# Eight weight chunks converted in the second stage of the last batch, one instruction per scheduler item

## The chip, the cores and the metric

The kernel runs on one core of a Trainium2 chip. TensorE (PE) multiplies matrices and loads its weights beside that (PEld); VectorE (DVE), ScalarE (ACT) and GpSimd (POOL) do the elementwise work; SyncE (SP) issues all the DMAs, in its program's order. Each engine works through its own instructions in order. The time of a run is the device time of the core in microseconds (us); lower is better.

## The reference, cut to what matters

Three layers follow each other. `B, S` are 4 and 576, the width is 512.

```python
# 1 attention: 4 batches, 8 heads, 1152 keys, 64 wide; queries pooled by two
q_pool = q.reshape(B, H, S // 2, 2, D).mean(axis=3)
attn = softmax(q_pool @ k.T / 8);  x = attn @ v
# 2 four experts, each a causal attention with one head; the two best by the gate are added
logits = x @ w_gate
out += gate[..., e] * (softmax(causal(x @ wq[e] @ (x @ wk[e]).T / 8)) @ (x @ wv[e]) @ wo[e])
# 3 feed-forward with a shifted input
xk = mu_k * x + (1 - mu_k) * x_prev;  xr = mu_r * x + (1 - mu_r) * x_prev
k = np.maximum(xk @ w_k, 0.0);  v = k * k @ w_v;  r = sigmoid(xr @ w_r)
out = r * v
```

`w_k` (512x1024), `w_r` (512x512) and `w_v` (1024x512) come as float64.

## The kernel before

Every matrix product is made of three: a float32 operand is split into a high part and a low part, and high x high, high x low and low x high are added in PSUM.

The float64 weights are first made into such pairs. `w3_split` cuts them into 20 chunks of 128x512 numbers: 8 of `w_k`, 4 of `w_r`, and 8 of `w_v`, which are numbers 12 to 19. A chunk is one load of 512 KB into a tile `w3st` (`ld`); seven DVE instructions and two ACT instructions that build the high and the low part from the bits (`sp1`, `sp2`; lines 884 to 902, with the copy and the difference in the helpers' lines 145 and 71); and two stores of 256 KB to DRAM, `w3h` and `w3l` (line 905). There is one `w3st` buffer, so the load of a chunk waits until both stores of the chunk before it have been read out.

The first part of the program runs the attention of 32 heads (8 a batch; `s1_job`, `s1_max`, `s1_prep`), and beside it the experts of the batch before (`s2_qk`, `s2_max`, `s2_job`, `s2_out`). The nth head of a batch always has the same second-stage work beside it. Then comes the second stage of the last batch, alone with the feed-forward of the first group of 256 rows (`s2_vproj`, the gate, `s2_qk`, `s2_job`, `h_steps`). Then the third stage goes through nine groups of 256 rows: `s3_h` (tile `sth`), `s3_r` (`str`), `s3_v` (`stw`). `s3_v` reads `w_v` from the tiles `wqk_h`, `wqk_l` and `XH`, `XL`, which hold other data until the second stage is over; rows 0 to 3 of `w_v` go to the first two, rows 4 to 7 to the other two, by `w3_load` (lines 1072 and 1073).

The order comes about in two steps. `drive` walks over steps and calls, between them, what each `Task` has due: a `Task` has a start, an end and a list of items, which are spread evenly between the two. What is recorded in that order is then ordered by a scheduler that fills an engine's free places with later work that is ready. So an item can stand well ahead of its place in the list, as far as its inputs and its buffer allow; and within one item nothing says that its instructions stay together.

The names of the second stage, in the order of its work: `stv` is the projection of the values, `stq` that of queries and keys (ACT and DVE make `QA`, `KA`, `QB`, `KB` from it; for every second expert these are the tiles `wvg_h`, `wvg_l`, `QB2b`, `KB2b`), `PM` the row maxima, `nm` their negative, `st` the scores, `p` their exponentials, `U` the sum over the values, `sd`, `rd`, `scr`, `R` the way of the softmax sum through DRAM and back, `YH` and `YL` the result, and `sto` its projection.

Of the kernel before, what the change touches and what calls it, by code (L numbers as in the profile page):

```python
# [55 lines left out]
def tile_kernel(ctx: ExitStack, tc: tile.TileContext, q, k, v, w_gate, wq, wk, wv, wo,  # L56
                mu_k, mu_r, w_k, w_v, w_r, out):
    nc = tc.nc
    LAG, LO, HB = G["LAG"], G["LO"], G["HB"]
    eng = {"g": nc.gpsimd, "v": nc.vector, "s": nc.scalar}  # L60

    def copy(e, dst, src):
        if e == "s":
            nc.scalar.activation(dst, src, AF.Copy)  # L64
        elif e == "v":
            nc.vector.tensor_copy(dst, src)
        else:
# [62 lines left out]
    def f32(ap):  # L130
        return ap.bitcast(F32)
# [12 lines left out]
    def act_hi(dst, src):  # L144
        nc.scalar.activation(dst, src, AF.Copy)
# [14 lines left out]
    def later(n, fn):  # L160
        pending.append((now[0] + n, fn))
# [82 lines left out]
    def normaliser(U, gate, name):  # L244
# [8 lines left out]
        def mid():  # L253
# [49 lines left out]
    def s2_gate(b):  # L303
# [3 lines left out]
        def f():  # L307
# [22 lines left out]
            def g():  # L330
# [247 lines left out]
    NF = G["NF"]  # L578
# [284 lines left out]
    CW = G["CW"]  # L863

    def w3_split(first, end, pool, bufs):
        def chunk(src, n):
            cell = {}

            def ld():
                t = pool.tile([P, max(1280, 5 * G["CW"])], F32, tag="wst", name=f"w3st{n}", bufs=bufs)  # L870
                cell["t"] = t
                if n < 2 and G["blk"]:
                    nc.gpsimd.tensor_copy(t[0:1, 0:1], XT[0:1, G["blk"] - 1, 0:1])
                nc.sync.dma_start(t[:, : 2 * CW].bitcast(I32), src.bitcast(I32))

            def sp1():
# [12 lines left out]
                nc.vector.tensor_scalar(si, ai, -0x800000, None, op0=ALU.bitwise_and)
                if G["wt"] == "g":  # L890
                    nc.gpsimd.tensor_scalar(s, s, 2.0**-36, 0.0, op0=ALU.mult, op1=ALU.add)
                    nc.gpsimd.tensor_tensor(s, low, s, op=ALU.mult)
                else:
                    nc.vector.scalar_tensor_tensor(s, low, 2.0**-36, s, op0=ALU.mult, op1=ALU.mult)
# [103 lines left out]
    n = len(steps)  # L998
# [201 lines left out]
    LAG, LO = G["L2"], G["O2"]  # L1200
# [27 lines left out]
    for e in range(E - 1):  # L1228
        i = ix[marks[e]]
# [59 lines left out]
```

## Time and profile before

| | |
|---|---|
| median of 3 runs | 1118.49 us (1116.62 to 1121.4) |
| the profiled execution | 1109.82 us |
| its span, first to last instruction | 1108.1 us |
| PE busy | 93% |
| DVE busy | 77% |
| ACT, POOL busy | 49%, 38% |
| mean granted TensorE clock | 0.991 |

The profiled execution is a single one, and 8.67 us below the median. Its stages, by the first instruction of each: the first part from 0 to 775 us, the second stage of the last batch to 861, the third stage to the end. PE and DVE are both almost always busy in the first part. In the third stage PE is busy without a break, and DVE half of the time.

### The profile page before, as it was taken

Reading aid. Unit: us, or ns where it says so; the run is one execution under the profiler, and the core shown is the slowest. Engines: PE = TensorE matmul, PEld = TensorE weight load, DVE = VectorE, ACT = ScalarE, POOL = GpSimd, SP = SyncE. Lnnn points to the kernel's source line nnn. Section 1 sums busy time; section 2 is a strip of 40 time slices with the busy share of each in tenths; the row PEclk is TensorE's granted clock in tenths of the full one; section 3 lists DMA queues with packets and bytes.
Section 4 is the critical chain, followed back from the end, with each engine's and each line's share of the span. In section 5 each row is a group of like instructions: output and inputs, shape, how many; then the busy total and the mean of one; then the engine's idle time right before and its main releaser. Section 6 shows DMA issues by size and latency. Waiting matters only on the chain.

```text
span 1108.1 us, 18899 instructions
## 1 busy us (share of the span) xinstructions
PE 1033.5 (93%) x6800; PEld 906.4 (82%) x6800; DVE 855.6 (77%) x1664; ACT 548.1 (49%) x922; POOL 420.7 (38%) x378
## 2 busy tenths in 40 slices
PE   5999999999999889999998889998999999999998
PEld 4788888888888888878878878886887888888887
DVE  5899998899889989999999989897555444444442
ACT  5567666556555455655655546656245212222222
POOL 7343328346444554453566346346100111111110
PEclk9999999999999999999999999999999999999999
DMA  4656545445544554545455445415405021111100
GB/s 113 149 151 145 128 114 128 100 128 153 129 109 116 152 135 125 149 134 135 100 143 158 126 116 130 127 54 182 150 1 182 31 81 39 39 39 39 39 20 20
DMA packets 129099, 119.29 MB, mean 108 GB/s; under 512 B 63751, under 2 KB 91358, under 8 KB 129006
## 3 DMA queue, kind: packets, MB, share of 16 engines
q1 hardware_dynamic: 129006, 118.08, 40.4%
q8 instruction: 54, 0.88, 0.3%
q14 instruction: 39, 0.32, 0.1%
HBM read 63.24 MB, written 20.07 MB: 75 GB/s over the span
## 4 chain that ended last, share of the span: by engine, by line
PE 56%; DVE 27%; DMA 7%; ACT 4%; issue 4%; POOL 1%; SPq 1%; DVEq 0%; ACTq 0%; POOLq 0%
PE stw L1122 9%; PE sth L1086 8%; DVE PM L732 7%; PE str L1109 5%; PE bank L730 5%; PE st L760 4%; PE st L761 4%; PE bank L795 3%; PE bank L797 3%; PE bank L796 3%; PE stq L354 3%; PE bank L788 2%; DVE pl L71 2%; PE bank L498 2%; DVE QA L151 1%
## 5 line engine op out<-in xcount | busy, mean ns | idle before, releaser
L71 POOL TENSOR_TENSOR pl<-p,ph 128x576 fp32r<-128x576 f32 x152 | 234.7, 1550 | 231.4 <-ACT ph L64 159.5
L732 DVE TENSOR_REDUCE PM<-bank 128x1 f32<-128x384 f32 (+1 forms) x480 | 251.9, 543 | 18.6 <-PE bank L730 15.0
L768 ACT ACTIVATE p<-st 128x576 f32<-128x576 f32 x288 | 185.6, 649 | 103.0 <-PE st L761 98.2
L730 PE MATMUL bank<-KA,QA 128*128 128x384 f32 (+1 forms) x480 | 180.4, 389 | 19.5 <-DVE PM L732 9.3
L64 ACT ACTIVATE ph<-p 128x576 fp32r<-128x576 f32 x238 | 162.7, 686 | 61.6 <-PE bank L796 51.9
L760 PE MATMUL st<-QA,KA 128*128 128x288 f32 x576 | 177.7, 319 | 4.5 <-ACT p L768 2.0
L761 PE MATMUL st<-QB,KB 65*128 65x288 f32 x576 | 167.3, 305 | 1.2 <-DMA QB<-mr 1.1
L797 PE MATMUL bank<-pl,VV 128*65 128x288 f32 x480 | 142.3, 297 | 8.4 <-DVE pl L71 6.1
L795 PE MATMUL bank<-ph,VV 128*65 128x288 f32 x480 | 144.7, 302 | 3.1 <-DVE PM L732 1.2
L796 PE MATMUL bank<-ph,VV 128*64 128x288 f32 x480 | 141.6, 295 | 0.0
L760 PEld LDWEIGHTS st<-QA,KA 128*128 128x128 f32 x576 | 111.0, 193 | 14.2 <-ACT p L768 5.6
L730 PEld LDWEIGHTS bank<-KA,QA 128*128 128x128 f32 (+1 forms) x480 | 87.4, 185 | 36.8 <-DVE PM L732 16.0
L761 PEld LDWEIGHTS st<-QB,KB 65*128 65x128 f32 x576 | 110.6, 193 | 4.1 <-DMA QB<-mr 2.0
L1025 POOL TENSOR_SCALAR yxr<-x,omr 128x256 f32<-128x256 f32 x36 | 25.6, 725 | 194.2 <-DVE xkl L151 136.0
L1086 PE MATMUL sth<-xkh,wk 128*128 128x256 f32 x512 | 90.9, 279 | 0.0
L1093 ACT ACTIVATE relu<-sth 128x512 f32<-128x512 f32 x32 | 17.4, 597 | 129.1 <-PE sth L1086 129.1
L71 DVE TENSOR_TENSOR pl<-p,ph 128x576 fp32r<-128x576 f32 x88 | 78.1, 888 | 1.6 <-ACT ph L64 0.7
L1086 PEld LDWEIGHTS sth<-xkh,wk 128*128 128x128 f32 x512 | 78.5, 188 | 0.4
L797 PEld LDWEIGHTS bank<-pl,VV 128*65 128x65 f32 x480 | 65.3, 136 | 12.6 <-DVE pl L71 7.7
L795 PEld LDWEIGHTS bank<-ph,VV 128*65 128x65 f32 x480 | 66.0, 138 | 7.9 <-DVE PM L732 3.0
L1086 PE MATMUL sth<-xkl,wk 128*128 128x256 f32 x256 | 71.4, 279 | 0.0
L796 PEld LDWEIGHTS bank<-ph,VV 128*64 128x64 f32 x480 | 65.2, 136 | 6.0
(209 smaller groups left out, 2336.5 us busy)
## 6 DMA issues: line engine op xcount, KB each, us to landing
KA<-sk SPq DMA_DIRECT2D x60, 160.0 KB
qr<-in_q_dram SPq DMA_DIRECT2D x32, 288.0 KB
kr<-in_k_dram SPq DMA_DIRECT2D x32, 288.0 KB
VF<-in_v_dram SPq DMA_DIRECT2D x32, 288.0 KB
KA<-sk SPq DMA_DIRECT2D x60, 128.0 KB
R<-scr SPq DMA_DIRECT2D x48, 144.0 KB
w3h<-w3st SPq DMA_DIRECT2D x20, 256.0 KB
w3l<-w3st SPq DMA_DIRECT2D x20, 256.0 KB
```

The lines of the kernel that those rows point to most:

```text
L64: nc.scalar.activation(dst, src, AF.Copy)
L71: eng[e].tensor_tensor(dst, src, hi.bitcast(F32), op=ALU.subtract)
L730: nc.tensor.matmul(ps[:n, : 3 * P], QA[i][:, t0 : t0 + n], KA[i][:, 3 * g * P : 3 * (g + 1) * P], start=True, stop=True)
L732: nc.vector.tensor_reduce(pm[:n, c, g : g + 1], ps[:n, : 3 * P], axis=AX.X, op=ALU.max)
L760: nc.tensor.matmul(st[:, n, :HT], KA[i][:, ks], QA[i][:, cs], start=True, stop=False)
L761: nc.tensor.matmul(st[:, n, :HT], KB[i][0 : D + 1, ks], QB[i][0 : D + 1, cs], start=False, stop=True)
L768: nc.scalar.activation(pt, st[:, :, :HT], AF.Exp, scale=1.0 / 16.0)
L795: nc.tensor.matmul(a[: D + 1, :HT], vh, ph[:, n], start=c == 0, stop=False)
L796: nc.tensor.matmul(a[:D, :HT], vl, ph[:, n], start=False, stop=False)
L797: nc.tensor.matmul(a[: D + 1, :HT], vh, pl[:, n], start=False, stop=c == NC - 1)
L1086: nc.tensor.matmul(st[:, f // 2, f % 2 * GT : (f % 2 + 1) * GT], w[kt][:, fs], x[:, kt], start=i == 0, stop=i == 3 * KT - 1)
L1122: nc.tensor.matmul(st[:, c], x[:, f, ts], w[f], start=i == 0, stop=i == 3 * FT - 1)
```

## The change

`w_v` is taken out of the first part's task, whose window stays as it is (12 chunks, from 7 steps into the second batch to 14 steps before the end). A new task in the last batch's second stage, between its steps 3 and 27, has the 8 chunks of `w_v`, with a `w3st` buffer in another pool. And `sp1` and `sp2` are cut into seven items, so that nearly every DVE instruction is an item of its own.

```diff
-G = {... 'w3d': 0, 'w3q': (0, 2.0), ...}
+G = {... 'w3d': 8, 'w3q': (3, 27), ...}
...
             def sp1():
+                t, high, low, a, s, r = parts()
                 nc.scalar.activation(r, high.bitcast(F32), AF.Square)
-                nc.vector.tensor_scalar(si, high, 0x07FFFFFF, 3, op0=ALU.bitwise_and, op1=ALU.logical_shift_left)
-                nc.vector.scalar_tensor_tensor(ai, high, -0x40000000, si, op0=ALU.bitwise_and, op1=ALU.bitwise_or)
+                nc.vector.tensor_scalar(s.bitcast(I32), high, 0x07FFFFFF, 3, op0=ALU.bitwise_and,
+                                        op1=ALU.logical_shift_left)
+            def sp2():
+                t, high, low, a, s, r = parts()
+                nc.vector.scalar_tensor_tensor(a.bitcast(I32), high, -0x40000000, s.bitcast(I32),
+                                               op0=ALU.bitwise_and, op1=ALU.bitwise_or)
+            def sp3():
+                t, high, low, a, s, r = parts()
                 nc.vector.scalar_tensor_tensor(a, r, TINY, a, op0=ALU.is_ge, op1=ALU.mult)
+                act_hi(r.bitcast(F32R), a)
...
-            return [ld, sp1, sp2]
+            return [ld, sp1, sp2, sp3, sp4, sp5, sp6, sp7]
```

What stands where is seen in the instructions' order. DVE, near the end of the first part (head 29 of 0 to 31; `pl` is a low part of the exponentials, `U1` a head's sum over the values). Before:

```order
L409 CAST mr2_2_2_9604<-bank762_9603 5x128
L71 TENSOR_TENSOR YL_158<-U2_2_1_9427,YH_157 64x576
L403 TENSOR_REDUCE nm1_30_9705<-PM0_196 128x5
L886 SCALAR_TENSOR_TENSOR w3st19_9639<-w3st19_9639 128x512
L887 SCALAR_TENSOR_TENSOR w3st19_9639<-w3st19_9639 128x512
L889 TENSOR_SCALAR w3st19_9639<-w3st19_9639 128x512
L894 SCALAR_TENSOR_TENSOR w3st19_9639<-w3st19_9639 128x512
L409 CAST mr1_30_9717<-bank769_9716 5x128
L71 TENSOR_TENSOR w3st19_9639<-w3st19_9639 128x512
L902 TENSOR_TENSOR w3st19_9639<-w3st19_9639 128x512
```

The same place of the changed kernel:

```order
L531 TENSOR_TENSOR U2_2_1_9330<-U2_2_1_9330,R2_2_1_9394 64x576
L732 TENSOR_REDUCE PM0_196<-bank767_9584 64x1
L732 TENSOR_REDUCE PM1_197<-bank768_9612 128x1
L71 TENSOR_TENSOR YL_158<-U2_2_1_9330,YH_157 64x576
L403 TENSOR_REDUCE nm1_30_9607<-PM0_196 128x5
L409 CAST mr1_30_9619<-bank769_9618 5x128
L71 TENSOR_TENSOR XL_151<-XT_161,XH_150 128x576 x2
```

The conversion is gone here. The scheduler brings the 12 chunks that are left forward: the last of them ends in head 24, so that heads 25 to 31 have none, and the heads before have nearly as many as before.

DVE in the second stage, between the second and the third expert's operands (`nm2_3_1` is the second expert's maximum, `U2_3_0` the first one's result, `QA2` and `KB2` the third one's operands). Before:

```order
L436 TENSOR_TENSOR PM2_164<-PM2_164 64x1
L381 TENSOR_REDUCE nm2_3_1_10802<-PM2_164 128x5
L142 TENSOR_SCALAR U2_3_0_10861<-bank821_10856,epsc_134 65x288
L151 TENSOR_TENSOR QA2_154<-stq3_2_10813,QA2_154 64x576
L151 TENSOR_TENSOR KB2_153<-stq3_2_10813,KA2_152 64x576
L142 TENSOR_SCALAR U2_3_0_10861<-bank822_10870,epsc_134 65x288
```

The changed kernel at that place:

```order
L436 TENSOR_TENSOR PM2_164<-PM2_164 64x1
L381 TENSOR_REDUCE nm2_3_1_10755<-PM2_164 128x5
L888 TENSOR_SCALAR w3st15_10636<-w3st15_10636 128x512
L142 TENSOR_SCALAR U2_3_0_10826<-bank821_10821,epsc_134 65x288
L893 SCALAR_TENSOR_TENSOR w3st15_10636<-w3st15_10636 128x512
L898 SCALAR_TENSOR_TENSOR w3st15_10636<-w3st15_10636 128x512
L904 TENSOR_SCALAR w3st15_10636<-w3st15_10636 128x512
L151 TENSOR_TENSOR QA2_154<-stq3_2_10770,QA2_154 64x576
L908 SCALAR_TENSOR_TENSOR w3st15_10636<-w3st15_10636 128x512
L71 TENSOR_TENSOR w3st15_10636<-w3st15_10636 128x512
L151 TENSOR_TENSOR KB2_153<-stq3_2_10770,KA2_152 64x576
L917 TENSOR_TENSOR w3st15_10636<-w3st15_10636 128x512
```

Chunk 15 stands here: its first instruction, which needs the chunk's load, ahead of `U2_3_0`, and four of its seven ahead of `QA2`.

PE at the end of the first group's `stw` (`stw0` has 48 matmuls, 24 for each half of its rows; `sth1_0` and `sth1_1` are the 96 of the next group's first product). Before, the 48 stand together, and `sth1_0` behind them:

```order
L1122 MATMUL stw0_11238<-XH_150,KH0_10350 128x512
L1122 MATMUL stw0_11238<-XH_150,KL0_10351 128x512
L1122 MATMUL stw0_11238<-XL_151,KH0_10350 128x512
L1086 MATMUL sth1_0_11291<-xkh1_11225,wk0_0_10145 128x256
L1086 MATMUL sth1_0_11291<-xkl1_11226,wk0_0_10145 128x256
L1086 MATMUL sth1_0_11291<-xkh1_11225,wk0_1_10146 128x256
```

In the changed kernel the last of the 96 stand ahead of the last 27 of `stw0`:

```order
L1101 MATMUL sth1_1_11350<-xkh1_11225,wk3_0_10047 128x256
L1101 MATMUL sth1_1_11350<-xkl1_11226,wk3_0_10047 128x256
L1101 MATMUL sth1_1_11350<-xkh1_11225,wk3_1_10048 128x256
L1137 MATMUL stw0_11238<-XH_150,KH0_10246 128x512
L1137 MATMUL stw0_11238<-XH_150,KL0_10247 128x512
L1137 MATMUL stw0_11238<-XL_151,KH0_10246 128x512
L1137 MATMUL stw0_11238<-wqk_h_146,KH0_10246 128x512
L1137 MATMUL stw0_11238<-wqk_h_146,KL0_10247 128x512
L1137 MATMUL stw0_11238<-wqk_l_147,KH0_10246 128x512
```

The first three `stw0` rows here read the last row of `w_v`, from chunk 19. The two high ones and the low one of chunk 18 stand farther up, among the `sth1` matmuls.

On SP the eight loads and sixteen stores of `w_v` stand among the second stage's own DMAs; the load of chunk 18 stands behind the first part of the third group's input (`x2_2`), and the load of chunk 19 behind the last expert's `scr`.

## Rows read from the trace of the kernel before

**Rows 1.** The page: busy us (share) by engine, and DVE's tenths by slice

```profile
PE 1033.5 (93%) x6800; PEld 906.4 (82%) x6800; DVE 855.6 (77%) x1664; ACT 548.1 (49%) x922; POOL 420.7 (38%) x378
DVE  5899998899889989999999989897555444444442
```

**Rows 2.** Windows: length, busy (instructions) PE, PEld, DVE, ACT, POOL, PEclk, DMA share, GB/s

```profile
571.00:734.00 163.00, 148.95 (x1040) 133.44 (x1039) 151.14 (x292) 91.41 (x155) 74.63 (x57) 0.99 0.49 129
775.00:861.00 86.00, 80.45 (x578) 70.32 (x579) 48.44 (x109) 35.68 (x63) 9.14 (x14) 0.98 0.35 110
```

**Rows 3.** Windows of `w3st` alone: length, its DVE, ACT, POOL, then as above

```profile
361.10:387.80 26.70, 4.85 (x6) 0.63 (x1) 0.00 (x0) 1.00 0.57 157
568.80:597.10 28.30, 6.44 (x7) 1.30 (x2) 0.00 (x0) 1.00 0.52 148
443.80:463.70 19.90, 3.94 (x6) 0.64 (x1) 0.00 (x0) 1.00 0.51 123
652.50:675.60 23.10, 5.82 (x6) 1.32 (x2) 0.00 (x0) 0.93 0.52 129
463.70:496.10 32.40, 9.96 (x14) 2.60 (x4) 0.00 (x0) 1.00 0.55 150
675.60:704.90 29.30, 4.86 (x8) 1.29 (x2) 0.00 (x0) 1.00 0.47 123
178.20:208.50 30.30, 2.81 (x5) 1.14 (x2) 0.71 (x1) 1.00 0.41 100
597.10:626.00 28.90, 8.11 (x10) 1.96 (x3) 0.00 (x0) 1.00 0.53 147
498.00:571.00 73.00, 12.39 (x14) 2.60 (x4) 0.00 (x0) 1.00 0.50 123
571.00:734.00 163.00, 33.94 (x42) 7.79 (x12) 0.00 (x0) 0.99 0.49 129
```

**Rows 4.** Waits, 571 to 734: waiter, what ended it, us, times, longest

```profile
PEld bank L730 <- DVE PM L732: 3.0, 3, 1.9
PE bank L730 <- DVE PM L732: 2.3, 2, 1.7
```

**Rows 5.** Tile `w3st`, 486 to 500: ns shortest/median/longest, first and last start

```profile
L874 SPq DMA_DIRECT2D w3st<-in_moe_w_r_dram x1: 339/339/339, 486.8 to 486.8; - x1
...
L885 DVE TENSOR_SCALAR w3st<-w3st x1: 418/418/418, 491.5 to 491.5; 128x512 int32<-128x512 int32 x1
...
L905 SPq DMA_DIRECT2D w3l<-w3st x1: 326/326/326, 496.0 to 496.0; - x1
L874 SPq DMA_DIRECT2D w3st<-in_moe_w_v_dram x1: 337/337/337, 498.7 to 498.7; - x1
```

**Rows 6.** Tile `w3st` over the whole span, one of its seven DVE lines

```profile
L885 DVE TENSOR_SCALAR w3st<-w3st x20: 404/428/1575, 81.9 to 719.8; 128x512 int32<-128x512 int32 x20
```

**Rows 7.** Timeline, DVE and SP: start, us, instruction, idle before and what ended it

```profile
777.70 0.33 SPq L1072 DMA_DIRECT2D wr_h<-w3h  x1
789.66 0.75 DVE L817 TENSOR_TENSOR XT<-U,R 64x576 f32<-64x576 f32 x1 [2.22 <-DMA R<-scr]
823.79 0.75 DVE L151 TENSOR_TENSOR QA<-stq,QA 64x576 fp32r<-64x576 f32 x1 [1.90 <-ACT QB L145]
```

**Rows 8.** Chain that ended last, in order of time: start, us, what

```profile
761.25 2.84 DMA wk<-w3l
...
861.53 11.20 PE stw L1122 x48
872.73 11.22 PE sth L1086 x96
...
889.62 1.86 PE sto L550 x12
```

**Rows 9.** Windows around a fall of the clock, columns as in rows 2

```profile
840.00:845.00 5.00, 2.88 (x21) 2.13 (x20) 3.20 (x8) 1.79 (x3) 0.00 (x0) 0.99 0.98 327
845.00:850.00 5.00, 5.00 (x20) 3.94 (x19) 4.24 (x10) 0.73 (x3) 2.18 (x4) 0.67 0.26 89
```

More of the change, by code (lines that the diff above doesn't have):

```diff
@@ L25 @@
 D = 64
-G = {'LAG': 4, 'LO': 2, 'nf1': 2, 'nfx': 1, 'mxA': (0, 5), 'prA': (0.5, 5.0), 'mx0': (-2.0, 7.0), 'mx1': (-2.5, 6.0), 'vl': (0.0, 1.5), 'vs': (5.5, 1.0), 'pr0': (0.5, 5.0), 'pr1': (0.5, 4.0), 'ld': (6.5, 5.5), 'm2': (2.0, 1.5), 'nm': 0, 'nm2': 0, 'dup': 2, 'mid': 1, 'bc': 1, 'end': 9, 'mid2': 2, 'end2': 4, 'spl': 9, 'gate': 8, 'gate2': 2, 'w2': (2, 30), 'w3': (7, 14), 'S0': ('n', 'sv', 'sg', 'n', 'sv', 'n', 'sv', 'sv', 'sv'), 'S1': ('sg', 'sg', 'sv', 'sg', 'sg', 'sg', 'sv', 'n', 'sg'), 've': 'g', 'kh0': 's', 'kh1': 'v', 'qh0': 's', 'qh1': 's', 'kq': 's', 'kl': 'v', 'rs': 'v', 'rl': 'v', 'ym': 'g', 'yo': 'v', 'LGe': 'v', 'p1': (5, 5, 5, 9), 'p2': (9, 9, 9), 'p3': (2,), 'p4': (9, 9, 9, 9), 'p5': (8, 8, 8, 8), 'p6': (9, 9, 9), 'po': (2, 4, 5, 9), 'add0': 'g', 'add1': 'g', 'xt': 'v', 'u1': 'v', 'u2': 'v', 'y2': 'v', 'yh': 's', 'yl': 'v', 'xo': 'v', 'v2': 's', 'xh': 'g', 'xl': 'v', 'vvh': 'g', 'vvl': 'g', 'klo': 'v', 'HB': 3, 'PB': 6, 'blk': 1, 'm2w': 2, 'order': 2, 'kdup': 0, 'L2': 4, 'O2': 1, 'a0': (5.0, 5.0), 'a1': (2.0, 2.5), 'a2': (0.0, 1.0), 'a3': (2.0, 2.0), 'r0': 2, 'NV': 2, 'NF': 2, 'SA': ('n', 'vg', 'sg', 'n', 'sv', 'n', 'sv', 'sv', 'sv'), 'SB': ('n', 'sv', 'sv', 'n', 'vv', 'n', 'sv', 'sv', 'sv'), 'ua': 'v', 'u0': 'v', 'xt0': 'v', 'w3d': 0, 'w3q': (0, 2.0), 'WC': 1, 'kb': 1, 'kst': 1, 'qst': 0, 'CW': 512, 'wt': 'v', 'wl': 'v', 'wa': 'v', 'WB': 1, 'mxg': 2, 'hq': 's', 'hpos': (0, 1, 11, 20)}
@@ new lines @@
+G = {'LAG': 4, 'LO': 2, 'nf1': 2, 'nfx': 1, 'mxA': (0, 5), 'prA': (0.5, 5.0), 'mx0': (-2.0, 7.0), 'mx1': (-2.5, 6.0), 'vl': (0.0, 1.5), 'vs': (5.5, 1.0), 'pr0': (0.5, 5.0), 'pr1': (0.5, 4.0), 'ld': (6.5, 5.5), 'm2': (2.0, 1.5), 'nm': 0, 'nm2': 0, 'dup': 2, 'mid': 1, 'bc': 1, 'end': 9, 'mid2': 2, 'end2': 4, 'spl': 9, 'gate': 8, 'gate2': 2, 'w2': (2, 30), 'w3': (7, 14), 'S0': ('n', 'sv', 'sg', 'n', 'sv', 'n', 'sv', 'sv', 'sv'), 'S1': ('sg', 'sg', 'sv', 'sg', 'sg', 'sg', 'sv', 'n', 'sg'), 've': 'g', 'kh0': 's', 'kh1': 'v', 'qh0': 's', 'qh1': 's', 'kq': 's', 'kl': 'v', 'rs': 'v', 'rl': 'v', 'ym': 'g', 'yo': 'v', 'LGe': 'v', 'p1': (5, 5, 5, 9), 'p2': (9, 9, 9), 'p3': (2,), 'p4': (9, 9, 9, 9), 'p5': (8, 8, 8, 8), 'p6': (9, 9, 9), 'po': (2, 4, 5, 9), 'add0': 'g', 'add1': 'g', 'xt': 'v', 'u1': 'v', 'u2': 'v', 'y2': 'v', 'yh': 's', 'yl': 'v', 'xo': 'v', 'v2': 's', 'xh': 'g', 'xl': 'v', 'vvh': 'g', 'vvl': 'g', 'klo': 'v', 'HB': 3, 'PB': 6, 'blk': 1, 'm2w': 2, 'order': 2, 'kdup': 0, 'L2': 4, 'O2': 1, 'a0': (5.0, 5.0), 'a1': (2.0, 2.5), 'a2': (0.0, 1.0), 'a3': (2.0, 2.0), 'r0': 2, 'NV': 2, 'NF': 2, 'SA': ('n', 'vg', 'sg', 'n', 'sv', 'n', 'sv', 'sv', 'sv'), 'SB': ('n', 'sv', 'sv', 'n', 'vv', 'n', 'sv', 'sv', 'sv'), 'ua': 'v', 'u0': 'v', 'xt0': 'v', 'w3d': 8, 'w3q': (3, 27), 'WC': 1, 'kb': 1, 'kst': 1, 'qst': 0, 'CW': 512, 'wt': 'v', 'wl': 'v', 'wa': 'v', 'WB': 1, 'mxg': 2, 'hq': 's', 'hpos': (0, 1, 11, 20)}
@@ L874, in ld, with parts @@
                 nc.sync.dma_start(t[:, : 2 * CW].bitcast(I32), src.bitcast(I32))
-            def sp1():
+            def parts():
                 t = cell["t"]
@@ L881, in sp1 @@
                 a, s, r = (t[:, (2 + i) * CW : (3 + i) * CW] for i in range(3))
-                ai, si = a.bitcast(I32), s.bitcast(I32)
+                return t, high, low, a, s, r
+            def sp1():
+                t, high, low, a, s, r = parts()
                 nc.scalar.activation(r, high.bitcast(F32), AF.Square)
-                nc.vector.tensor_scalar(si, high, 0x07FFFFFF, 3, op0=ALU.bitwise_and, op1=ALU.logical_shift_left)
-                nc.vector.scalar_tensor_tensor(ai, high, -0x40000000, si, op0=ALU.bitwise_and, op1=ALU.bitwise_or)
@@ L887, in sp1 @@
-                nc.vector.scalar_tensor_tensor(a, r, TINY, a, op0=ALU.is_ge, op1=ALU.mult)
[L889 to L894, printed above, removed]
@@ L896, in sp2 @@
-            def sp2():
-                t = cell["t"]
-                a, s, r = (t[:, (2 + i) * CW : (3 + i) * CW] for i in range(3))
+                nc.vector.tensor_scalar(s.bitcast(I32), high, 0x07FFFFFF, 3, op0=ALU.bitwise_and,
[4 more added lines that the diff above has]
+                                               op0=ALU.bitwise_and, op1=ALU.bitwise_or)
@@ new lines, in sp3, with sp4, sp5 @@
+            def sp3():
+                t, high, low, a, s, r = parts()
+                nc.vector.scalar_tensor_tensor(a, r, TINY, a, op0=ALU.is_ge, op1=ALU.mult)
+                act_hi(r.bitcast(F32R), a)
+            def sp4():
+                t, high, low, a, s, r = parts()
+                nc.vector.tensor_scalar(s.bitcast(I32), a.bitcast(I32), -0x800000, None, op0=ALU.bitwise_and)
+            def sp5():
+                t, high, low, a, s, r = parts()
+                nc.vector.scalar_tensor_tensor(s, low, 2.0**-36, s, op0=ALU.mult, op1=ALU.mult)
@@ L899, in sp2, with sp6, sp7 @@
+            def sp6():
+                t, high, low, a, s, r = parts()
+                lo_of(G["wl"], a, a, r.bitcast(F32R))
+            def sp7():
+                t, high, low, a, s, r = parts()
                 hi, lo = r.bitcast(F32R), s.bitcast(F32R)
-                act_hi(hi, a)
-                lo_of("g" if G["wt"] == "g" else G["wl"], a, a, hi)
-                eng["g" if G["wt"] == "g" else G["wa"]].tensor_tensor(lo, a, s, op=ALU.add)
+                eng[G["wa"]].tensor_tensor(lo, a, s, op=ALU.add)
```

## The prediction

> **What bounds the kernel now.** I read the page first: PE is busy 93% of the span, DVE 77%, but DVE's slices stand at 8 and 9 up to the thirtieth and at 4 and 5 behind it [rows 1]. So the share hides two regimes, and I cut the span into windows. In the heads that the change empties (571 to 734 us) DVE is busy 151.14 of 163 us, 93%, and PE shows 148.95 [rows 2]; the waits of that stretch name DVE's row maxima ahead of PE's score matmuls [rows 4]. There DVE is the scarcer engine, and PE waits for its queue more than for its work. In the second stage of the last batch (775 to 861 us) DVE is busy only 48.44 of 86 us and POOL 9.14 [rows 2]. That is room, but not free room: the stage is a chain PE, ACT, DVE, PE, expert after expert, in which `QA` starts as soon as ACT is done [rows 7], so what stands ahead of such a link on DVE moves PE. Behind 861 us PE runs without a gap through `stw` and `sth` [rows 8].
>
> **Part 1: what leaves the first part.** Eight chunks are 56 DVE instructions, 16 on ACT, 8 loads and 16 stores. The DVE part is 12.39 + 33.94 = 46.3 us, the last two rows of their group [rows 3]. ACT's part (about 1.3 us a chunk, 10.4 in all) and the DMAs lie beside other work there, ACT being busy 91 of 163 us [rows 2]; I count them at nothing, and if that cover failed the loss would already be in the head times below. How much of 46.3 us comes back as time? The nth head of each batch has the same other work, so heads of one kind with more and with less conversion can be compared, two rows to a pair [rows 3]. First heads: 1.59 us more conversion, 1.60 us longer. Fourth heads: 1.88 more, 3.20 longer, of which the clock of 0.93 takes 23.1 x 0.07 = 1.6. Fifth heads: 5.10 more, 3.10 longer. Second heads: 5.30 more, 1.40 shorter. The first three kinds together: (1.60 + 1.60 + 3.10) / (1.59 + 1.88 + 5.10) = 0.735 us per us; the second kind nothing. Eight kinds take equal turns, and some are like each; I take 0.5, between the ends 0 and 0.735 and nearer the three. Gain 46.3 x 0.5 = 23.2 us, with ends 0 and 34. Most of it should come in heads 25 to 29, where no chunk is left by the order, since the 12 others are brought forward.
>
> **Part 2: what the second stage gets.** Its clock is the chunk chain with one buffer. In a quiet stretch the first DVE instruction starts 491.5 - 486.8 = 4.7 us after the load is issued, the low part's store is issued 496.0 - 491.5 = 4.5 us after that, and the next load 498.7 - 496.0 = 2.7 us later: 11.9 us a chunk [rows 5]. On DVE the order sets other instructions between the seven: for chunk 15 they are one `U`, `QA` and `KB`, some 2.0 us with 0.75 for a 64x576 [rows 7]; for others less. I take 1.6 more: 13.5 us a chunk. The bounds for that surplus are 0 and 4.
>
> The first load can go where the first `wr_h` load goes, 777.7 [rows 7], since its buffer lies in memory that the first part has just left. Its chunk's last instructions stand behind `XT` and `XL`, and `XT` waits for a DMA until 789.66 [rows 7]; with the rows between, the low store goes at about 795, and the second load at 797.6. Six more cycles put the load of chunk 19 at 797.6 + 6 x 13.5 = 878.6. Add 4.7, 4.5 and 2.0 for what stands between: store at 889.8, landed 2.7 later at 892.5. Then the load into `XL`, 2.84 us like a 256 KB load in the first part [rows 8]: 895.3. PE has by then done all it can: 18 of `stw0` and the 96 of `sth1`, which the new order sets ahead. From the low `XL` matmul on 25 are left, at 11.20 / 48 = 0.233 us [rows 8], 5.8 us: `stw0` ends at 901.1. Before, `sto` followed at 889.62, 5.7 us behind the end of `sth` at 883.95 [rows 8], because squares and copies of `sth1` came in between. These are half done by then in the new order; I take 3.0 us. So `sto` starts at 904.1 instead of 889.62: a loss of 14.5 us.
>
> The DVE chain says much the same in another way. Conversion stands ahead of `QA` of the first and third expert, of `nm`, and of every second expert's operands: for chunk 15 four instructions, some 2.2 us at the shortest durations, and the load's landing. With about 1.3 us for each of five links that is 6.5 us until `stw0` can start, so PE's own bound for `sto` is 861.5 + 6.5 + 22.4 + 3.0 = 893.4, 3.8 us late. If nothing were held up, `sto` would come 2.7 us early, since only the gap shrinks. Ends of this term: -2.7 and 14.5 + 6 x 2.4 = 29.
>
> Queues that the chunks are moved past: on SP a load that waits for its buffer holds the DMAs behind it, among them `sd` and `R` of the experts; these end in `YH` and `YL`, which are first read by `sto`, so they have some 50 us. ACT gets 10.4 us where it is busy 35.68 of 86; its copies stand between `KA` and `QA`, within the 1.3 us above. The transfers, 8 x 1 MB, go where the DMA share is 0.35 [rows 2]. POOL gets nothing.
>
> **Sum.** -23.2 + 14.5 = -8.7 us on the profiled execution's 1109.82 us. The median of the runs is 8.67 above that execution; I take the difference over to it: 1118.49 - 8.7 = 1109.8, said as 1110.
>
> **Rivals.** (a) *The chain keeps up.* The loads land early enough and PE's own bound holds: 3.8 instead of 14.5, so -19.4, 1099. For it: DVE has 37 free us in the stage. Against it: one buffer, and 11.9 us at the very least.
>
> (b) *The `w_v` chain sets the end; slower than before.* Each further us on a chunk's cycle counts six times. The load of chunk 18 stands on SP behind an input that needs DVE's last `yxr`, and the load of chunk 19 behind `scr`, which needs the last `rd`: SP may hold both for some us each, and PE stands still in `stw0`. At a cycle of 16.5 us it is 18 us more: +9.3, 1128. It decides from 15.0 (no gain left), and shows as slower from 15.9.
>
> (c) *Part of what leaves was never DVE's work.* An instruction of line 885 takes 0.404 us at its shortest and 1.575 at its longest [rows 6], while POOL is busy 74.63 of 163 us in the emptied heads and 9.14 of 86 in the second stage [rows 2]. If the long ones wait for POOL, and other instructions of DVE wait there instead once these have gone, only 8 x 4.5 = 36 us leave: gain 18, sum -3.5, 1115. [...]
>
> (d) *PE's clock falls at the new waits.* After a stretch with PE busy 2.88 of 5 us the granted clock was 0.67 in the next 5 us, a loss of 5 x 0.33 = 1.65 us [rows 9]. PE now waits up to four times for rows of `w_v`; two such falls are 3.3 us: -5.4, 1113. [...]
>
> **How the numbers follow.** Chances: forecast 0.36, (a) 0.20, (b) 0.20, (c) 0.14, (d) 0.10. Of this kernel a measurement can tell about 0.5%, 5.6 us. The forecast's own range is 1104 to 1116, three quarters of it faster by more than that; (a) is faster; (b) is slower in 0.17 and the same in 0.03; (c) is the same but for 0.02; (d) is the same in 0.06 and faster in 0.04. Faster 0.27 + 0.20 + 0.02 + 0.04 = 0.53, same 0.09 + 0.03 + 0.12 + 0.06 = 0.30, slower 0.17. The range goes to 1095, where (a) meets the better end of the gain, and to 1126, short of (b)'s price: about 0.2 is left out.
>
> **What would show it.** In the profile of the changed kernel: heads 25 to 29 shorter by some 14 us together, DVE there under 88%, and PE's waits on `PM` fewer; if they last as long as before, Part 1 fails. The loads of `w_v` 12 to 15 us apart; the first `stw` at 6 to 7 us more behind the first `stv`; PE idle among the first `sth` matmuls of the third stage, ended by DMAs into `XH` and `XL`; `sto` 14 us later against the stage's start. If PE shows no such idle time, (a) is right; if the loads are 16 us apart, (b). Conversion at 4.3 to 4.5 us a chunk in the new place, with the head times hardly shorter, would speak for (c).

## The result, and the profile after

The changed kernel took 1108.51 us (median of 6 runs, 1103.22 to 1112.98), the kernel before 1117.62 us beside it (6 runs, 1114.54 to 1123.99): a ratio of 0.9881 with an interval of 0.9841 to 0.9922, 1.2% faster. The two medians by themselves divide to 0.9918 (9.1 us), which lies in the same interval.

The two profiled executions don't show this gain: they took 1109.82 us before and 1109.79 us after. The one of before lay below every later run of that kernel, the one of after near its median. So the two traces show well how time moves inside the program, and the medians show how much is gained.

The page of the kernel after, the lines that answer to [rows 1] (busy us and share by engine, and DVE's tenths in 40 slices):

```profile
PE 1031.3 (93%) x6800; PEld 908.1 (82%) x6800; DVE 843.1 (76%) x1664; ACT 550.4 (50%) x922; POOL 414.4 (37%) x378
DVE  5899998789999888989987877885777624444442
```

DVE's work is now spread more evenly: most of the slices from the twenty-second on fell from 9 to 7 and 8, those of the second stage rose from 5 to 7. Heads 25 to 29 by themselves, before (length, busy us and instructions of PE, PEld, DVE, ACT, POOL, then PE's granted clock, DMA share, GB/s):

```profile
597.10:733.90 136.80, 127.24 (x890) 113.36 (x889) 125.54 (x251) 78.04 (x133) 62.04 (x47) 0.99 0.48 125
```

The same five heads after, and the second stage of the last batch in the window of [rows 2]:

```profile
586.90:715.20 128.30, 123.75 (x889) 112.07 (x888) 98.64 (x214) 72.39 (x123) 58.78 (x46) 1.00 0.37 90
775.00:861.00 86.00, 74.87 (x496) 62.63 (x497) 64.52 (x144) 38.03 (x69) 7.25 (x9) 0.94 0.45 143
```

The heads lost 27 us of DVE's work and 8.5 us of time; the first experiment's trace shows below that this trace of before was slow in them. In the second stage DVE does 16 us more than in [rows 2] in the same window, PE 5.6 us less, and the clock is 0.94. The waits of PE on DVE's row maxima in the emptied heads (568 to 727 us; waiter, what ended it, us, times, longest), which answer to [rows 4]:

```profile
PEld bank L730 <- DVE PM L732: 0.7, 2, 0.5
PE bank L730 <- DVE PM L732: 0.2, 1, 0.2
```

They have nearly gone. For the second stage I measure from the last `stv` matmul to the last `sto` matmul. In the kernel before (ns shortest/median/longest, first and last start, forms):

```profile
L287 PE MATMUL stv<-wvg_l,XH x20: 278/283/291, 792.2 to 799.0; 128*128 128x260 f32 x16, 128*64 128x260 f32 x4
L550 PE MATMUL sto<-YH,wo_h x16: 293/296/398, 883.8 to 890.9; 128*128 128x288 f32 x16
L550 PE MATMUL sto<-YH,wo_l x16: 293/296/298, 884.0 to 891.2; 128*128 128x288 f32 x16
```

The last `stv` there starts at 799.0 us; `sto` begins at 883.8, and its last matmul starts at 891.2, 92.1 us behind that `stv` (92.15 before rounding). After:

```profile
L287 PE MATMUL stv<-wvg_l,XH x20: 280/283/420, 776.6 to 785.0; 128*128 128x260 f32 x16, 128*64 128x260 f32 x4
L550 PE MATMUL sto<-YH,wo_l x16: 293/296/298, 884.6 to 891.0; 128*128 128x288 f32 x16
L874 SPq DMA_DIRECT2D w3st<-in_moe_w_v_dram x8: 333/336/457, 760.9 to 860.8; - x8
L888 DVE TENSOR_SCALAR w3st<-w3st x8: 417/428/499, 766.4 to 865.3; 128x512 int32<-128x512 int32 x8
L920 SPq DMA_DIRECT2D w3l<-w3st x8: 319/320/382, 779.5 to 872.2; - x8
```

`stv` ends 14.0 us earlier and the stretch is 106.0 us, 13.8 longer; from the last `sto` to its end PE needs 212.3 us in both. So in these two executions the first part gives 14 us and the second stage takes the same 14 back.

Where do the 13.8 us arise? I numbered PE's matmuls behind the last `stv` and compared their start times; the table is worked out from the traces (us behind the last `stv`; five, seven and eight are the numbers of `w_v` chunks in the second stage, and "raw apart", "one load" and "early", which the experiments explain, hold eight too). The order of PE's instructions differs a little between the kernels, so a row compares progress and not always the same matmul.

| matmul | before | loads only | five | seven | eight (after) | raw apart | one load | early |
|---|---|---|---|---|---|---|---|---|
| 100th | 13.5 | 13.5 | 14.4 | 14.4 | 14.4 | 21.0 | 18.5 | 19.0 |
| 300th | 40.4 | 40.4 | 44.2 | 44.6 | 44.5 | 57.5 | 51.9 | 56.3 |
| 375th | 56.5 | 57.2 | 56.9 | 58.8 | 58.7 | 70.2 | 66.2 | 72.2 |
| 425th | 65.8 | 66.5 | 67.1 | 73.1 | 74.3 | 81.9 | 75.5 | 84.9 |
| 500th | 78.4 | 79.1 | 79.7 | 85.6 | 85.2 | 94.5 | 88.1 | 97.5 |
| 550th | 84.3 | 84.9 | 85.5 | 91.5 | 98.3 | 100.3 | 94.0 | 103.8 |
| 600th | 92.0 | 92.7 | 93.3 | 99.2 | 105.9 | 108.1 | 101.7 | 111.5 |

After is 4.1 us late at the 300th matmul, as five is too, and makes most of this up; then it is 2.2 us late at the 375th, 8.5 at the 425th, and 14.0 at the 550th: in the main two places, not a steady loss. Both stand in its chain of waits (start, us, what). The first is at chunk 18:

```profile
844.61 0.49 DVE yxr L1042
...
845.12 0.37 SPq L1031
...
845.59 0.80 DMA w3st<-in_moe_w_v_dram
846.38 3.62 issue
...
850.57 0.66 ACT p L482
...
851.27 4.39 PE bank L498 x10
```

SP issues the chunk's load at 845.6, when DVE's last `yxr` has let a DMA ahead of it go. That holds the load for some 0.6 us only: the chunk before issues its low store at 843.0, and with one buffer the loads of chunks 13 to 16 too came 2.0 us behind such a store. The Square waits on ACT until 850.0, and the exponentials `p`, whose scores PE had delivered, stand behind it in ACT's order. PE waits 3.9 us for `p`, and its clock falls to 0.50 in the next 5 us, as the windows show (columns as before):

```profile
845.00:850.00 5.00, 2.40 (x18) 1.67 (x16) 2.13 (x4) 1.35 (x3) 0.00 (x0) 0.94 0.71 220
850.00:855.00 5.00, 3.73 (x10) 1.83 (x11) 4.62 (x10) 2.40 (x5) 3.10 (x4) 0.50 0.30 101
```

The second place is the end of the chain of chunks, which `stw` needs:

```profile
860.83 4.35 DMA w3st<-in_moe_w_v_dram
...
872.21 2.04 DMA w3l<-w3st
874.26 2.49 DMA XL<-w3l
876.80 6.22 PE stw L1137 x19
```

PE waits 2.67 us there for `XL`, and its clock in the next 5 us, 875 to 880, is 0.67. Both kinds of loss can be told apart over the whole stretch, from the last `stv` to the last `sto` matmul (length, busy us of PE, PEld, DVE, ACT, POOL, PE's clock, DMA share, GB/s): before, after, and the kernels of the columns "raw apart", "one load" and "early".

```profile
799.00:891.20 92.20, 87.89 (x604) 76.00 (x603) 50.68 (x112) 38.20 (x65) 7.70 (x12) 0.98 0.22 71
785.00:891.00 106.00, 92.09 (x604) 77.15 (x603) 78.91 (x163) 46.34 (x79) 8.75 (x12) 0.95 0.42 131
785.60:893.80 108.20, 94.97 (x603) 81.41 (x602) 76.29 (x161) 46.06 (x79) 10.24 (x12) 0.91 0.37 124
784.40:886.20 101.80, 93.18 (x603) 79.58 (x602) 76.27 (x160) 45.93 (x78) 8.36 (x12) 0.93 0.30 100
790.50:902.20 111.70, 100.67 (x604) 85.80 (x603) 74.23 (x158) 45.23 (x77) 7.99 (x12) 0.86 0.36 119
```

The matmuls are the same. After, PE is busy 4.2 us longer, at a mean clock of 0.95 instead of 0.98, and idle 9.6 us longer. With the early window it is the other way round: 12.8 us longer busy, at 0.86, and 6.7 us longer idle.

### The profile page after: what moved, and what is told of

Same layout as the page of the kernel before. It is cut to its first block, busy times and chain, and to the rows that moved or that the text cites. A ratio compares the mean times of both kernels' runs of the same rounds, so it can differ in the third digit from the quotient of the medians.

```text
span 1108.0 us, 18910 instructions
## 1 busy us (share of the span) xinstructions
PE 1031.3 (93%) x6800; PEld 908.1 (82%) x6800; DVE 843.1 (76%) x1664; ACT 550.4 (50%) x922; POOL 414.4 (37%) x378
## 4 chain that ended last, share of the span: by engine, by line
PE 62%; DVE 21%; DMA 8%; ACT 4%; issue 3%; SPq 1%; POOL 1%; DVEq 0%; ACTq 0%; POOLq 0%
PE stw L1137 9%; PE sth L1101 7%; PE bank L730 6%; PE st L760 5%; DVE PM L732 5%; PE st L761 4%; PE str L1124 4%; DMA R<-scr 4%; PE bank L797 3%; PE bank L795 3%; PE bank L796 3%; PE bank L788 3%; PE stq L354 3%; PE bank L498 3%; DVE pl L71 2%
## 5 line engine op out<-in xcount | busy, mean ns | idle before, releaser
L71 POOL TENSOR_TENSOR pl<-p,ph 128x576 fp32r<-128x576 f32 x152 | 230.6, 1521 | 208.9 <-ACT ph L64 115.7
L730 PE MATMUL bank<-KA,QA 128*128 128x384 f32 (+1 forms) x480 | 177.8, 383 | 13.7 <-DVE KB L151 4.4
L760 PEld LDWEIGHTS st<-QA,KA 128*128 128x128 f32 x576 | 110.9, 193 | 12.5 <-ACT p L768 4.0
```

The lines of the kernel that those rows point to most:

```text
L730: nc.tensor.matmul(ps[:n, : 3 * P], QA[i][:, t0 : t0 + n], KA[i][:, 3 * g * P : 3 * (g + 1) * P], start=True, stop=True)
L760: nc.tensor.matmul(st[:, n, :HT], KA[i][:, ks], QA[i][:, cs], start=True, stop=False)
```

## The experiments

Twelve kernels ran, each beside the kernel before; ratios are to it, with their intervals.

**Is it the move or the finer items?** The first kernel keeps all 20 chunks in the first part and has only the finer items; the second moves eight chunks with the three old items.

```diff
-'w3d': 8, 'w3q': (3, 27)      # e1, in the kernel after
+'w3d': 0, 'w3q': (3, 27)
-'w3d': 0, 'w3q': (0, 2.0)     # e2, in the kernel before
+'w3d': 8, 'w3q': (3, 27)
```

> All 20 chunks stay in the first part, only cut into the finer items. Theory A (the place of the w_v chunks decides): no change, ratio to before 0.997 to 1.003. Theory B (the finer items decide, since single DVE instructions fill gaps that a bunch cannot): 0.985 to 0.992, most of the change's gain.

> The w_v chunks move to the second stage, in the old three items a chunk. Theory A: as the change, ratio 0.984 to 0.992. Theory B: little is left, 0.997 to 1.005, since bunches of four DVE instructions now stand ahead of QA and nm, and the second stage loses over 20 us instead of 15.

Measured: 1122.08 us, 1.0009 (0.9985 to 1.0033), and 1109.02 us, 0.9899 (0.9878 to 0.9921). The finer items do nothing by themselves; the move is the whole gain. The planner runs in steps, and at three steps a chunk several of its eight items fall into one step; that splitting them therefore moves few instructions is likely, but not shown. The first kernel's trace also shows the work of before at its usual time: `stv` ends at 810.6 us, the stretch to the last `sto` is 92.8 us. Against this trace the changed kernel reaches its last `stv` 25.6 us earlier. Heads 16 to 24 and 25 to 29 of the first kernel, and heads 16 to 24 of the changed one (columns as before):

```profile
362.20:609.60 247.40, 224.13 (x1496) 194.91 (x1496) 224.63 (x427) 132.06 (x224) 118.50 (x86) 0.98 0.50 130
609.60:743.30 133.70, 126.47 (x889) 113.80 (x889) 123.71 (x251) 78.14 (x133) 63.73 (x47) 0.99 0.49 128
356.90:586.90 230.00, 214.44 (x1493) 190.61 (x1492) 209.55 (x412) 131.07 (x219) 117.46 (x87) 1.00 0.50 130
```

Heads 16 to 24 lose 19.5 us of conversion on DVE and become 17.4 us shorter; heads 25 to 29 lose 26.4 us of it and become 5.4 us shorter (133.7 to 128.3). In these five heads PE had only 7.2 us without work. The trace of the fourth kernel (below), with the same 20 chunks in the first part, gives 13.7 and 4.3 us. So most of the gain lies ahead of the heads that the change empties.

**What is each part worth?** One kernel leaves the conversion of `w_v` out altogether and reads other converted rows in its place; another converts all 20 chunks in the first part and the eight of `w_v` once more in the second stage.

```diff
-w3_split(W3 // CW - G["w3d"], W3 // CW, s3, G["WC"])   # e3: task gone, loads read chunk wn % 12
-w3_split(0, W3 // CW - G["w3d"], s1a, G["WB"])         # e4
+w3_split(0, W3 // CW, s1a, G["WB"])
```

> The eight w_v chunks are converted nowhere (their rows are read from chunks 0 to 7, so the last product is made with other numbers); everything else as in the changed kernel. It shows the first part's gain by itself. Theory A: 23 us less than before, ratio 0.976 to 0.983, the second stage as long as before (about 92 us from the first stv to the first sto). [...]

> All 20 chunks in the first part, and the eight of w_v a second time in the second stage: the loss by itself. Theory A: the second stage 15 us longer (107 us instead of 92 from the first stv to the first sto), ratio 1.011 to 1.016. Rival (the second stage hides the conversion, and what the two profiles show there is chance): under 5 us, ratio under 1.005.

Measured: 1094.58 us, 0.9777 (0.975 to 0.9805): 25 us for the first part. And 1132.23 us, 1.0122 (1.0092 to 1.0152): 13.7 us for the second stage; in its trace the stretch is 105.2 us, 12.5 more than in the first experiment. -25 + 13.7 = -11.3, close to the change itself.

**What in the second stage costs it?** Three kernels: the raw words in a buffer of their own, so that a load need not wait for the stores before it; one load for all eight conversions; loads and stores without conversion (the output of the last two isn't the reference's).

```diff
+t = pool.tile([P, 2 * CW], F32, tag="wraw", ...)    # e5
+if pool is not s1a and n > 12: cell["t"] = keep[0]; return   # e6, in ld
+if pool is not s1a: return [ld, raw_out]            # e7
```

> As the changed kernel, but a w_v chunk's raw words have a buffer apart from its three work areas (same memory in all), so that the next load waits for the last read of the raw words and not for both stores. If the loss of the second stage (13.7 us by the run with both) is mostly the chain of load, conversion and store with one buffer, the cycle falls from 12 to 15 us to about 9 and PE no longer waits for rows of w_v in the first stw: 5 to 9 us less than the changed kernel, ratio to before 0.980 to 0.984. If the loss is DVE's 34 us of conversion ahead of the chain's links, nothing changes or it gets worse, 0.988 to 0.994, since the conversion is only packed closer.

> As the changed kernel, but the second stage loads only the first of its eight chunks and converts it eight times (rows 1 to 7 of w_v are then wrong); all conversions and stores stay. What the loads cost: if the chain with one buffer is the loss, 6 to 9 us less than the changed kernel, ratio to before 0.980 to 0.983; if it is the conversion itself, within 3 us of the changed kernel, 0.986 to 0.990.

> As the changed kernel, but the second stage's chunks are loaded and stored again without any conversion (the rows of w_v are then raw halves of float64). What the DMAs cost without the 56 DVE and 16 ACT instructions: if the conversion's DVE time is the loss, the second stage is as long as before, ratio to before 0.977 to 0.981; if the chain of DMAs were it, 0.984 to 0.988.

Measured: 1112.58 us, 0.9896 (0.9872 to 0.9921); 1106.4 us, 0.9853 (0.9819 to 0.9887); 1095.94 us, 0.9747 (0.9721 to 0.9773). The transfers by themselves cost nothing: the "loads only" column of the table never leaves "before" by more than 0.7 us, and the ratio of this kernel lies below its range. So it takes the conversion to lose time. But the first of the three contradicts the theory that one buffer is its cause: the last low store goes at 855.1 instead of 872.2 us, and the stretch is still 108.2 us; its ratio is the one expected for DVE's conversion ahead of the links. Its chain of waits shows why, early in the stage:

```profile
789.36 4.06 DMA w3l<-w3st
...
793.58 0.69 ACT w3st L893
...
796.27 0.65 ACT QB2b L145
...
798.27 0.77 DVE KB2b L151
799.06 0.69 DVE w3st L914
...
800.97 0.61 DVE w3st L923
801.59 2.72 DMA w3l<-w3st
...
804.44 0.43 DVE w3st L894
804.87 0.08 DVE nm L381
...
804.99 0.64 PE bank L386 x5
```

ACT's Square waits for the low store of the chunk before, since the work areas still have one buffer, with the attention's operands behind it. On DVE the conversion's instructions then stand between `wvg_l`, `KB2b`, the row maxima and `nm`, and the next chunk's first one, ahead of `nm`, waits 0.4 us for the next low store. Between 785 and 812 us PE waits 3.6 us for that `nm` (waiter, what ended it, us, times, longest):

```profile
ACT w3st L893 <- DMA w3l<-w3st: 6.2, 2, 5.0
PE bank L386 <- DVE nm L381: 3.6, 1, 3.6
```

Between 800 and 805 us PE is busy 0.40 us, and in the next 10 us its clock is 0.50.

The second kernel, with one load, came out between its two ranges, at 0.9853, and its stretch is 101.8 us, 9.6 more than before. It is 5.0 us late at the 100th matmul already. What its conversion waited for of DMAs in the whole stage (what ended it, us, times):

```profile
  DMA w3l<-w3st: 1.0, 3
  DMA w3st<-in_moe_w_v_dram: 0.3, 1
```

So 9.6 us are lost with next to no wait for a transfer: from 791.3 to 801.2 us six conversion instructions, 3.4 us, stand on DVE between `QA` and the expert's `nm`, PE is busy 3.2 to 4.0 of each 5 us from 790 to 805, and from 800 to 810 us its clock is 0.59 and 0.50. A chain packed closer puts more of the conversion, with whatever it waits for, ahead of the first links of the attention.

**How many chunks fit?** With the same three planner steps for each chunk I moved five, six and seven, and moved the window of the eight forward by three steps.

```diff
-'w3d': 8, 'w3q': (3, 27)
+'w3d': 5, 'w3q': (3, 18)      # e8
+'w3d': 6, 'w3q': (3, 21)      # e9
+'w3d': 7, 'w3q': (3, 24)      # e10
+'w3d': 8, 'w3q': (0, 24)      # e11
```

> As the changed kernel, but five chunks move instead of eight, between steps 3 and 18 of the second stage; 15 stay in the first part. Gain in the first part 5/8 of 25 = 15.7 us if it goes with the amount. If the second stage's loss is the end of the chunk chain, it is nearly gone (under 5 us) and this beats the changed kernel: ratio to before 0.984 to 0.990. If the loss goes with the amount as well (8.6 us), the ratio is 0.993.

> Six chunks of w_v in the last batch's second stage (planner window (3, 21), the same three steps for a chunk), fourteen in the first part. Measured from the last stv matmul to the last sto matmul the second stage took 92.2 us before, 106.0 with eight chunks, 93.4 with five. Theory A (only the tail costs: with eight chunks the loss sits where chunks 18 and 19 are converted, 7 us when ACT's Square waits for chunk 18's load with exponentials behind it and 7 to 8 us when chunk 19's store ends after stw wants XL): with six both are gone, the stretch takes 92 to 95 us, and the ratio to the kernel before is 0.979 to 0.983 (five gave 0.9828; one chunk less in the first part is worth 3.1 us or 0.3%). Rival B (every chunk past what fits costs alike, 13.8 us over three chunks): 97 to 99 us and a ratio of 0.983 to 0.986. Rival C (the sixth chunk takes up the last of DVE's room and pays as much as it brings): 95 to 97 us, 0.982 to 0.984.

> Seven chunks of w_v in the second stage (window (3, 24)), thirteen in the first part. Theory A (the tail): chunk 18 of eight is now the last, at the place where chunk 17's successor waited, so one of the two late places stays: 95 to 101 us from the last stv to the last sto matmul, ratio 0.979 to 0.985. Rival B (4.6 us for each chunk past five): 101 to 103 us, 0.984 to 0.988.

> Eight chunks as in the changed kernel, with the planner's window moved from (3, 27) to (0, 24), three steps or some 10 us earlier, and nothing else. Theory A (the chain of eight ends too late): its last store goes from 872 us to about 862 us, stw finds XL in time, and the stretch from the last stv to the last sto matmul is 96 to 100 us instead of 106; ratio 0.980 to 0.985. Rival D (what costs is any load of w_v that an instruction on ACT or DVE waits for ahead of the attention's own links, wherever the window lies): the loss moves to the front of the stage, as in the run with the raw words apart, where the 100th PE instruction after stv came 7.5 us late: 103 to 108 us, ratio 0.987 to 0.991.

Measured: five 1104.86 us, 0.9828 (0.9801 to 0.9855); six 1099.25 us, 0.9819 (0.978 to 0.9857); seven 1106.03 us, 0.9854 (0.9822 to 0.9887); eight, early, 1119.27 us, 0.9992 (0.9969 to 1.0015). Five chunks lengthen the stretch by 1.3 us only (93.4), and their ratio is a little better than the range said. Seven make it 99.4: the table shows the first place of the eight (7.3 us late at the 425th matmul) and not the second. That is the stretch that the theory of the tail had said; the ratio, 0.9854, lies in the rival's range. The early window falls against that theory: its last low store goes at 875.4, not at 862 us, the stretch is 111.7 us, and the lateness begins at the 100th matmul, as rival D said, and goes beyond its numbers. But waits for loads are not what it shows there: from 798 to 808 us the seven instructions of one conversion stand on DVE among `KB`, `wvg_l`, `KB2b` and the row maxima, and none of them waits for a load. PE is busy 1.99 us from 805 to 810, and the next 10 us run at 0.50 and 0.57. Another 5.5 us of this kernel's time lie ahead of its last `stv` (790.5 us, after 785.0); what they come from is not shown.

Six was expected at 92 to 95 us by the tail; the profiled execution, the slowest of the six runs (1108.75; the others 1096.0 to 1103.6), shows 99.0, while the ratio of all six is that of the tail. The two traces part at one point. Five chunks (windows, columns as before):

```profile
816.00:820.00 4.00, 3.42 (x21) 1.99 (x20) 3.54 (x7) 3.90 (x8) 0.00 (x0) 1.00 0.00 0
820.00:825.00 5.00, 4.80 (x34) 3.87 (x35) 4.91 (x10) 0.65 (x1) 0.00 (x0) 1.00 0.28 105
```

Six chunks, at the same work:

```profile
816.00:820.00 4.00, 1.74 (x14) 1.45 (x13) 2.62 (x6) 2.77 (x6) 0.00 (x0) 0.97 0.00 0
820.00:825.00 5.00, 5.00 (x22) 4.01 (x21) 4.49 (x8) 1.37 (x3) 0.00 (x0) 0.50 0.26 100
825.00:830.00 5.00, 5.00 (x24) 4.37 (x23) 3.25 (x10) 0.00 (x0) 0.00 (x0) 0.50 0.34 111
```

Here a chunk's load took 5.1 us from its issue to the first instruction that uses it (3.6 with five). PE worked 1.7 us less in the first window, and its clock was then 0.50 for 10 us, where it stayed at 1.00 with five. The 250th matmul came at 41.3 instead of 36.1 us: a wait of 1.7 us has become 5. Five, six and seven overlap in their intervals. All three are faster than the kernel before; against the changed kernel (0.9841 to 0.9922) five and six have the better ratios and lower medians, but the intervals still touch.

**Does it help to take the Square off ACT?** In the kernel with seven the Square of the second stage runs on POOL.

```diff
-nc.scalar.activation(r, high.bitcast(F32), AF.Square)
+nc.gpsimd.tensor_tensor(r, high.bitcast(F32), high.bitcast(F32), op=ALU.mult)   # e12, second stage
```

> The kernel with seven chunks (e10), whose second-stage Square runs on POOL as a multiplication instead of on ACT; nothing else. In e10 the 400th PE instruction after the last stv matmul came 5.7 us later than before, behind chunk 19's Square that waited 3.1 us for its load with the exponentials p behind it on ACT (bank L498 waited 3.6 us for p), and the stretch to the last sto matmul took 99.2 us. Theory A (ACT's queue: what a Square that waits for its load holds up is the loss): the 400th PE instruction comes within 2 us of its place before, the stretch is 92 to 95 us, the ratio to the kernel before 0.978 to 0.982. Rival E (the same load is waited for by DVE's first conversion instruction too, and the links behind that one are as late): the stretch stays at 97 to 101 us and the ratio at 0.983 to 0.988. [...]

Measured: 1109.94 us, 0.989 (0.9857 to 0.9924), the stretch 102.7 us. The cure fails, and the numbers lie past those of theory A and of rival E. What ACT shows at the first place (start, us, instruction, idle before and what ended it):

```profile
848.58 0.63 ACT L145 ACTIVATE w3st<-w3st 128x512 fp32r<-128x512 f32 x1 [5.57 <-POOL yxr L1043]
849.23 1.28 ACT L1130 ACT_TABLE_LOAD   x1
850.52 1.02 ACT L1130 ACTIVATE XT<-str 128x1024 f32<-128x1024 f32 x1
```

And DVE in the same microseconds:

```profile
844.36 0.43 DVE L891 TENSOR_SCALAR w3st<-w3st 128x512 int32<-128x512 int32 x1 [1.70 <-DMA w3st<-in_moe_w_v_dram]
844.70 1.59 DVE L71 TENSOR_TENSOR YL<-U,YH 64x576 fp32r<-64x576 f32 x1
...
847.82 0.68 DVE L901 SCALAR_TENSOR_TENSOR w3st<-w3st 128x512 f32<-128x512 f32 x1
```

The chunk's next ACT instruction, the copy, now heads the queue and waits for L901 of DVE, the third conversion instruction behind the load, which ends at 848.5; `XT` and PE's scores stand behind it. (The timeline names POOL there, but POOL's multiplication had ended at 845.7.) The wait in order moved from one ACT instruction to the next. The multiplication on POOL has its part as well: `YL` took 1.59 us beside it, and two of the seven instructions of line 896 took 1.41 and 1.10 us beside others, where one alone takes 0.68. That is some 2 us on DVE in a stretch that grew by 3.4; the two causes were not separated.

## Why the prediction was right

1110 us were forecast and 1108.51 measured; by differences -8.7 us were forecast, the medians differ by -9.1 us, and the measured ratio is -13.3 us of 1117.62 (8.7 to 17.8). Both parts of the sum came out near their sizes, but each with luck in it.

**The first part was sized well, and placed too narrowly.** 46.3 us of DVE at 0.5 were to give 23.2; the third experiment measured 25, 0.54 for each us. The factor came from heads of one kind with more and with less conversion, and it held as a mean only: against the first experiment's trace a us of conversion gave back 0.9 us in heads 16 to 24 and 0.2 in heads 25 to 29. That 0.5 lay between the two was luck. "Most of it should come in heads 25 to 29", some 14 us, was wrong: they gave 8.5 by the trace of before, and 5.4 by the first experiment's (DVE 77% there, under the 88% that I named). The twelve chunks that are left end at 565 us, where the eight of `w_v` had begun at 498.7 [rows 5], so the heads ahead of these five get less conversion too. In the third experiment, with no conversion of `w_v` at all, the five heads take 128.1 us, no less than here.

**The second stage: the sum was right, half of its mechanism was.** 14.5 us were forecast; 13.7 by the fourth experiment, 13.8 in the two profiles. Against the first `stv` the last low store was forecast at 889.8 - 791.9 = 97.9 us and came at 872.2 - 776.2 = 96.0; a chunk in 13.5 us, measured 12.0 to 15.2 behind a first cycle of 20.6. The loads are 12 to 15 us apart, and `sto` is 16 us later against the first `stv` where I said 14; the wait for `XL` stands in `stw`, not among the first `sth`, and the first `stw` is 9.5 us later and not 6 to 7. `XL` and `stw` did end last. But this place is worth 5.5 us only (from 8.5 late to 14.0). The other 8.5 are lost ahead of it, 6.3 of them at the load of chunk 18. I had SP's hold behind DVE's last `yxr` in rival (b), as a stretch of the cycle; it was 0.6 us, and the price was another, the exponentials behind ACT's Square. And the step "the DVE chain says much the same", with 3.8 us as the price if the chunks come early, was far too low: with the chunks earlier (one load, raw apart, early) the stage lost 9.6, 16.0 and 19.5 us. I priced the instructions in front of the links by their length, 1.3 us a link. I left out the transfer that the first of them waits for, which is the loss at chunk 18, and PE's clock, which fell behind such a delay, to 0.50 behind chunk 18: PE's own work took 4.2 us longer after, and 5.3, 7.1 and 12.8 us longer in those three.

**A misread row.** I took 889.62 of [rows 8] as the start of `sto`. It is the last of the stretches that the chain names; `sto` begins at 883.8 us, right behind `sth`. The gap of 5.7 us that I let shrink to 3.0 didn't exist. Measured from its true start, my sum would have been 901.1 - 883.8 = 17.3 us, 2.8 larger, and the forecast 1112.6. So a part of the agreement with the 13.8 is luck, and the 3.8 us above, which use the same gap, should have been 6.5.

**The rivals.** (a), the chain keeps up, falls: 13.7 us were lost. (b), slower, falls; its critical cycle of 15.0 was reached once, at 15.2. (c), that a part of what leaves was a wait for POOL, falls by the third experiment: 25 us, not 18. A longer DVE instruction beside POOL is seen once the Square runs there: with the multiplication on POOL from 844.42 to 845.68 us, DVE's `YL` beside it took 1.59 us, 0.84 more than an `XT` of the same size [rows 7]. Why it takes longer no run shows.

(d), that the clock falls at the new waits, is confirmed, beside the forecast: 0.50 at 850 to 855 us, after 5 us with PE busy 2.40, and 0.50 for 10 us with six chunks, where [rows 9] had 0.67 once. I priced two falls at 3.3 us; after, PE was busy 4.2 us longer. The long fall with six chunks cost an estimated 3.5, the 5 less the wait itself, and the early window 12.8 in all.

## What to carry to other kernels

When work is moved into idle time of an in-order engine, price what stands behind it in that engine's order: the moved instructions' own length ahead of each link, the transfer that the first of them waits for, and the clock that PE loses behind the delay. Here the clock was, by PE's busy time, some 4 of 14 us with the chosen window and 13 of 20 with the early one. Look for the point where the room ends: five of eight chunks cost the stage 1.3 us, the last one alone 6.6 (99.4 to 106.0), where a chunk brings an estimated 3.1 (25 us for eight). Start times of the same engine's nth instruction, set against each other, find such a point in two traces at once. A conversion that sits ahead of another engine's work returned about half of its DVE time in all, but 0.2 to 0.9 of it by place: compare the heads that fill as well as the heads that empty.

## What was not expected of the hardware

The kernel before spread over 1114.54 to 1123.99 us beside the changed kernel, and one execution took 1109.82: of the 12.4 us between the first trace and that of the first experiment 11.5 lie in the first part (the last `stv` at 799.0 and 810.6), and of these 11.4 in heads 16 to 24 (236.0 and 247.4 us). What decides this stays open. And behind 1.7 us less of PE's work in 4 us, 1.74 with six chunks against 3.42 with five, PE's clock was 0.50 for 10 us, where with five it stayed at 1.00.
